# Retention and two feed-forward layers: another load order, other group sizes, and products of zeros between the first blocks

## The chip, the cores and the metric

The kernel runs on one core of a Trainium2 chip. The metric is the device time of one execution in microseconds (us), from repeated runs; the median of three before the change is 877.78 us. A profile of one further execution gives the rows below.

## The reference

```python
scores = scale * np.matmul(q, k.transpose(0, 1, 3, 2))      # q, k, v: 4 x 8 heads x 576 x 64
Dmat = np.where(rel >= 0, gamma[:, None, None] ** rel[None, :, :], 0.0)
x = np.matmul(scores * Dmat[None], v)                       # retention
x = x.transpose(0, 2, 1, 3).reshape(2304, 512)
h = x @ w_in;  x = (h * sigmoid(h)) @ w_out                 # 512 -> 2048 -> 512
h = x @ w_in2; x = (np.maximum(h, 0) + alpha * np.minimum(h, 0)) @ w_out2
```

Everything is float32, but the four weight matrices come as float64.

## The kernel before, in words

**Retention** goes in 18 blocks of 128 tokens, each in two halves of 64 (`att_step`, line 521). A block is loaded in two transfers of 512 KB (`att_load`): q and k, then k and v by token. They go into a ring of five buffers, two of which lie in the buffer `sums` and three in `pack`. `att_prep` scales q and v by powers of gamma, on POOL or VectorE. `att_half` multiplies k with q into the PSUM pair `sc`, and k with v into the running state `total`, in products of 64 x 64 that use a quarter of the array each; the state is copied out after each half (`att<-total`). `att_mask` multiplies `sc` with a mask on VectorE (`att<-sc`, once for each block). `att_out` multiplies states with q and masked scores with v into `xo`; a copy makes the rounded half `xhi` of it and a subtraction the rest, `xlo`.

**The layers** work on products of a rounded high part and a rest: three matmuls for one exact product. A weight tile (512 KB of float64) is loaded into one of two `raw` buffers by `weight` (line 383), and split there by two ScalarE conversions (`top`, `low`), five VectorE instructions, a ScalarE cast and a POOL product (`low<-low,top`). The 2048 hidden features are 16 tiles, taken in groups (`SIZES`, line 31). For each group and each of five token tiles (256, then 512 four times) there are h units (`h_unit`: 12 matmuls into one of three `bank` buffers, then sigmoid or relu, and the split of the result) and, in the first layer, four y units (`y_unit`: three matmuls for each tile of the group, added into `sums` by VectorE from the second group on; in the layer's last group a rounded part and a rest of the sum are made too). The second layer has `out_unit` in place of y.

**The order** of instructions is not that of the code. `Program` records all operations, and `order` lists them with estimated costs: the operation of an engine that is ready and has to be done first (`late`) goes first; TensorE's work is in two queues, retention and layers, whose units stay whole. The result is a fixed order for each engine, and an engine stands still while its next instruction waits. `first` (line 651) puts the blocks between the units of the first group: 6 blocks ahead of the first h unit, the others spread over the rest. The order is issued in two parts, cut at `close_att`; the weights of the first group and of two tiles of the second one belong to the first part.

`gate` (line 374) copies one column of `src` into a buffer about to be loaded, so that the load waits until `src` is there. It holds back blocks 1 to 4 and the first two weights. Before the first block TensorE multiplies zeros (`WARM`, line 33).

Of the kernel before, what the change touches and what calls it, by code (L numbers as in the profile page):

```python
# [18 lines left out]
P = 128  # L19
# [8 lines left out]
NCH = S // C  # L28


SIZES = [[1, 3, 4, 4, 4], [4, 4, 4, 4]]
GROUPS = [(i, range(sum(sizes[:n]), sum(sizes[:n + 1]))) for i, sizes in enumerate(SIZES) for n in range(len(sizes))]
WARM = 12
LEAD = 4
TILES = [256, 512, 512, 512, 512]
RAWS = 2
# [19 lines left out]
class Program:  # L56
# [19 lines left out]
    def __init__(self, nc):  # L76
        self.nc = nc
        for name in self.ENGINES:
            setattr(self, name, self.Engine(self, name))
        self.ops, self.first = [], 0  # L80
        self.writer, self.readers, self.banks = {}, {}, {}
        self.end = {}
        self.free = dict.fromkeys(self.LATENCY, 700.0)
        self.dma, self.was, self.started = 0.0, None, []
        self.queue, self.units, self.joined = "layers", 0, False

    def unit(self, queue, joined=False):

# [19 lines left out]
    def cost(self, engine, out, reads):  # L108
        n = int(np.prod([c for _, c in out.ap[1:]]))
        psum = any(r.space == bass.MemoryType.PSUM for r in reads)  # L110
        if engine == "PE":
            return (n + 32) / 2.4 if reads[0].dtype == F32R else 29 if n == C else 3.4 * n
        if engine == "ACT":
            return (160 if psum else 200) + 0.84 * n + 50 * any(r.dtype != F32 for r in reads)
        if engine == "DVE":
            return 140 + (0.56 if len(reads) < 2 and not psum else 1.075) * n
        if engine == "POOL":
            return 100 + 2.1 * n
        return 450

    def record(self, name, method, args, kwargs, others=()):
        engine = self.ENGINES[name]
        aps = {k: a for k, a in [*enumerate(args), *kwargs.items()] if isinstance(a, bass.AP)}
        key = "out" if "out" in aps else 0
        out = aps.pop(key)
        reads = list(aps.values())
        on_chip = lambda a: type(a.tensor).__name__ == "Tile"
        deps = set()
        i = len(self.ops)
        psum = {}  # L130
        for ap, writes in [(r, False) for r in reads] + [(out, True)]:
            if not on_chip(ap):
                continue
            if ap.space == bass.MemoryType.PSUM:

                for g in self.grains(ap):
                    psum[g] = True
                continue
            for g in self.grains(ap):
                if g in self.writer:  # L140
                    deps.add(self.writer[g])
                if writes:
                    deps.update(self.readers.pop(g, ()))
                    self.writer[g] = i
                else:
                    self.readers.setdefault(g, []).append(i)
        for g in psum:
            runs = self.banks.setdefault(g, [])
            if not runs or runs[-1][0] != engine:
                runs.append((engine, []))  # L150
            if len(runs) > 1:
                deps.update(runs[-2][1])
            runs[-1][1].append(i)
            del runs[:-2]
        deps.discard(i)
        moved = int(np.prod([c for _, c in out.ap])) * np.dtype(mybir.dt.np(out.dtype)).itemsize if engine == "SP" else 0
        shared = engine == "DVE" and all(r.space != bass.MemoryType.PSUM for r in reads)
        self.ops.append((engine, name, method, args, kwargs, deps, self.cost(engine, out, reads), moved,
                         shared, (self.queue, self.units, self.joined),
                         [(self.ENGINES[a], a, b, self.cost(self.ENGINES[a], out, reads)) for a, b in others]))  # L160

    def order(self):

# [7 lines left out]
                at += ops[i][6]  # L171
        for i in reversed(new):
            if ops[i][0] != "PE":
                late[i] = min(late[i], at)
            for d in ops[i][5]:
                if d >= self.first and ops[d][0] != "PE":
                    lag = self.LATENCY[ops[d][0]] if ops[d][0] != ops[i][0] else 0
                    late[d] = min(late[d], late[i] - ops[d][6] - lag)
# [101 lines left out]
def retention_ffn_kernel(ctx: ExitStack, tc: tile.TileContext, qkv, w1, w2, alpha, small, out):  # L280
# [89 lines left out]
    def psum():  # L370

        return rings["bank"].next()

    def gate(dst, src):

        nc.vector.tensor_copy(dst[:, 0:1], src[:, 0:1])


    w_hi, w_lo = {}, {}

    def weight(layer, kind, f):
        if (layer, kind, f) in w_hi:
            return
        raw, top, low, a, hi, lo = (rings[k].next() for k in ("raw", "top", "low", "a", f"w{kind}", f"w{kind}"))
        if len(w_hi) < RAWS:
            gate(raw.bitcast(F32), fac[:, 0])
        nc.sync.dma_start(out=raw, in_=(w1, w2)[layer][kind, f])
        words = raw.bitcast(I32).rearrange("p (n two) -> p n two", two=2)  # L390
        lower, upper = words[:, :, 0], words[:, :, 1]
        nc.scalar.activation(top, upper.bitcast(F32), AF.Copy, scale=2.0 ** -112)
        nc.scalar.activation(low, lower.bitcast(U32), AF.Copy, scale=2.0 ** -52)
        nc.vector.tensor_scalar(out=a, in0=top.bitcast(I32), scalar1=3, scalar2=None, op0=ALU.logical_shift_left)
        nc.vector.scalar_tensor_tensor(out=a, in0=top.bitcast(I32), scalar=-2 ** 31, in1=a, op0=ALU.bitwise_and,
                                       op1=ALU.bitwise_or)
        nc.vector.tensor_scalar(out=top.bitcast(I32), in0=a, scalar1=-2 ** 23, scalar2=None, op0=ALU.bitwise_and)
        nc.scalar.copy(hi, f32(a))
        nc.gpsimd.tensor_tensor(out=low, in0=low, in1=top, op=ALU.mult)
        nc.vector.tensor_tensor(out=f32(a), in0=f32(a), in1=f32(hi), op=ALU.subtract)  # L400
        nc.vector.tensor_tensor(out=lo, in0=f32(a), in1=low, op=ALU.add)
        w_hi[layer, kind, f], w_lo[layer, kind, f] = hi, lo

# [15 lines left out]
        return pack(n)[:, i].rearrange("p (c t) -> p c t", c=NPAIR)  # L421

    def att_load(n):
        if 1 <= n < PACKS:
            for i in (0, 2):
                gate(pack(n)[:, i], fac[:, 0] if n == 1 else pack(n - 2)[:, i + 1])
        nc.sync.dma_start(out=pack(n)[:, 0:2], in_=qkv[n, :, 0:2])
# [93 lines left out]
    def att_step(n):  # L521
# [3 lines left out]
        if m < NBLK:  # L525
            att_load(m)
            att_prep(m)
            att_half(m, 0)
        next(out)
        if m < NBLK:  # L530
            att_half(m, 1)
            att_mask(m)
        for _ in out:
            pass
# [106 lines left out]
            else:  # L641
                e()


    zero = rings["act"].tiles[0]
    nc.gpsimd.memset(zero, 0.0)
    nc.unit("retention")
    for _ in range(WARM):
        nc.tensor.matmul(total[:, 0:P], zero[:, 0:P], zero[:, P:2 * P], start=True, stop=True, skip_group_check=True)
    att_step(-1)  # L650
    first = [(s, u) for s in range(len(TILES)) for u in hs[s] + ys[s]]
    at = 0
# [80 lines left out]
```

## Time and profile before

| | us |
|---|---|
| three timed runs | 876.64, 877.78, 880.19 |
| the profiled execution | 879.05 |
| its span, first to last instruction | 877.2 |
| TensorE busy (PE) | 850.3 (97%) |
| VectorE busy (DVE) | 549.0 (63%) |
| ScalarE busy (ACT) | 380.5 (43%) |
| GpSimd busy (POOL) | 136.5 (16%) |

PE's busy time is taken from records that overlap, so busy is not the same as at its peak. The profile also names, for each 40th of the span, the clock that TensorE was granted: the lower level is half of the upper one. The rows that matter are in the section after the next.

### The profile page before, as it was taken

How to read it: one execution, taken by the hardware profiler on the slowest of the kernel's cores; microseconds unless marked ns; L12 is line 12 of the kernel's file. 1: busy time of each engine (PE TensorE's matmuls, PEld its weight loads, DVE VectorE, ACT ScalarE, POOL GpSimd, SP SyncE). 2: the span in 40 equal slices, each digit the busy share in tenths (PEclk: the TensorE clock that was granted, in tenths of full speed). 3: DMA queues.
4: the chain of work that ended last, by engine and by line, in shares of the span. 5: the costliest groups of instructions: out<-in, count | busy, mean ns of one | idle time of the engine just before them, and what ended most of it. 6: DMA issues, size and time to landing. Idle time of an engine off the chain costs nothing.

```text
span 877.2 us, 14384 instructions
## 1 busy us (share of the span) xinstructions
PE 850.3 (97%) x5956; PEld 715.2 (82%) x5956; DVE 549.0 (63%) x863; ACT 380.5 (43%) x711; POOL 136.5 (16%) x101
## 2 busy tenths in 40 slices
PE   6788999999999999999999999999999999999998
PEld 6666788888888888888888888888888888888887
DVE  4786499783369633995569832984369733954342
ACT  3354474352235422553346644763345533533340
POOL 3575022120003200220002200220002200200000
PEclk6799999999999999999999999999999999999999
DMA  8876032220012100320012100220012100101102
GB/s 310 298 262 206 2 121 73 67 78 1 0 49 96 49 1 0 97 97 1 1 48 97 49 1 1 97 96 1 1 49 97 48 1 1 49 1 48 49 25 96
DMA packets 17490, 58.30 MB, mean 66 GB/s; under 512 B 2064, under 2 KB 2448, under 8 KB 17424
## 3 DMA queue, kind: packets, MB, share of 16 engines
q1 hardware_dynamic: 17424, 57.38, 19.1%
q8 instruction: 46, 0.75, 0.4%
q14 instruction: 20, 0.16, 0.1%
HBM read 52.66 MB, written 4.72 MB: 65 GB/s over the span
## 4 chain that ended last, share of the span: by engine, by line
PE 91%; DVE 4%; issue 2%; DMA 1%; POOL 0%; ACT 0%; SPq 0%; POOLq 0%; DVEq 0%; ACTq 0%
PE bank L276 86%; DVE a L276 2%; PE xo L276 2%; PE sc L276 1%; PE total L276 1%; DMA sums<-in_qkv 1%; DVE act L276 1%; DMA pack<-in_qkv 1%; DVE att L276 0%; DVE xlo L276 0%; DVE top L276 0%; DVE gb L276 0%; POOL pack L276 0%; DVE w L276 0%; DVE g L276 0%
## 5 line engine op out<-in xcount | busy, mean ns | idle before, releaser
L276 PE MATMUL bank<-xhi,w 128*128 128x512 f32 (+1 forms) x880 | 252.0, 371 | 0.7 <-DVE w L276 0.7
L276 POOL TENSOR_TENSOR low<-low,top 128x512 f32<-128x512 f32 x64 | 95.7, 1501 | 600.9 <-DVE top L276 590.7
L276 PEld LDWEIGHTS bank<-xhi,w 128*128 128x128 f32 x880 | 160.7, 190 | 29.0 <-DVE w L276 1.0
L276 PE MATMUL bank<-xlo,w 128*128 128x512 f32 (+1 forms) x440 | 162.9, 370 | 0.0
L276 DVE TENSOR_TENSOR sums<-bank,sums 128x512 f32<-128x512 f32 (+1 forms) x135 | 88.1, 652 | 99.1 <-PE bank L276 98.5
L276 ACT ACTIVATE act<-bank 128x512 f32<-128x512 f32 (+1 forms) x160 | 88.3, 552 | 109.5 <-PE bank L276 105.4
L276 PE MATMUL bank<-xhi,w0b 128*128 128x512 f32 (+1 forms) x400 | 113.2, 368 | 0.0
L276 DVE SCALAR_TENSOR_TENSOR act<-down,nalpha_sb,act 128x512 f32<-128x512 f32 (+1 forms) x80 | 60.2, 753 | 80.0 <-ACT act L276 78.3
L276 PEld LDWEIGHTS bank<-xlo,w 128*128 128x128 f32 x440 | 83.7, 190 | 14.0
L276 ACT ACTIVATE down<-bank 128x512 f32<-128x512 f32 (+1 forms) x80 | 44.3, 554 | 103.7 <-PE bank L276 103.4
L276 PEld LDWEIGHTS bank<-xhi,w0b 128*128 128x128 f32 x400 | 72.6, 188 | 12.6
L276 DVE TENSOR_TENSOR act<-bank,act 128x512 f32<-128x512 f32 (+1 forms) x80 | 50.7, 633 | 50.4 <-ACT act L276 50.3
L276 PE MATMUL bank<-xlo,w0b 128*128 128x512 f32 (+1 forms) x200 | 73.6, 368 | 0.0
L276 DVE TENSOR_TENSOR gb<-act,gb 128x512 fp32r<-128x512 f32 (+1 forms) x79 | 51.9, 659 | 23.4 <-ACT gb L276 23.3
L276 ACT CAST g<-act 128x512 fp32r<-128x512 f32 (+1 forms) x81 | 47.4, 586 | 41.0 <-DVE act L276 41.0
L276 ACT ACTIVATE top<-raw 128x512 f32<-128x512 f32 x64 | 43.3, 676 | 49.7 <-POOL low L276 46.8
L276 PE MATMUL bank<-g,w 128*128 128x512 f32 (+1 forms) x280 | 63.7, 371 | 0.6 <-DVE act L276 0.6
L276 PE MATMUL bank<-gb,w1b 128*128 128x512 f32 (+1 forms) x304 | 62.3, 356 | 0.0
L276 PE MATMUL bank<-w1b,gb 128*128 128x512 f32 (+1 forms) x268 | 62.0, 380 | 0.2 <-DVE gb L276 0.2
L276 ACT CAST gb<-act 128x512 fp32r<-128x512 f32 (+1 forms) x79 | 44.9, 569 | 39.6 <-DVE act L276 39.6
L276 PEld LDWEIGHTS bank<-gb,w1b 128*128 128x128 f32 x304 | 50.7, 189 | 8.2
L276 PEld LDWEIGHTS bank<-w1b,gb 128*128 128x128 f32 x268 | 48.6, 188 | 10.2 <-DVE gb L276 0.6
(74 smaller groups left out, 1189.4 us busy)
## 6 DMA issues: line engine op xcount, KB each, us to landing
raw<-in_w SPq DMA_DIRECT2D x64, 512.0 KB, 3.5
pack<-in_qkv SPq DMA_DIRECT2D x22, 512.0 KB, 5.7
sums<-in_qkv SPq DMA_DIRECT2D x14, 512.0 KB, 5.4
out<-sums SPq DMA_DIRECT2D x17, 256.0 KB, 2.0
out<-sums SPq DMA_DIRECT2D x2, 128.0 KB, 1.7
att<-in_small SPq DMA_DIRECT2D x1, 214.0 KB, 2.6
alpha_sb<-in_alpha SPq DMA_DIRECT2D x1, 8.0 KB, 7.1
```

What stands on the lines that cost most here:

```text
L276: getattr(getattr(self.nc, name), method)(*args, **kwargs)
```

## The change

- **Groups.** The first layer's 16 tiles go in groups of 1, 2, 3, 4, 4 and 2 instead of 1, 3, 4, 4 and 4.
- **Products of zeros.** 36 of 64 columns instead of 12 of 128 ahead of the first block, and four more behind each half of blocks 0 and 1. They read the first `act` buffer and write the third `bank`. The planner counts 110 ns for one.
- **Loads.** The first weight (number 0) is no longer held and gets a due time that puts it first (`DUE`); number 1 is held until block 0's k has landed and is due at 6 us in the planner's time; numbers 2 to 7 are held until `xlo` of blocks 5, 6, 8, 9, 11 and 12 is out (`HOLD`, `LATER`).
- **Gates** are ScalarE copies instead of VectorE copies.

```diff
@@ -28,9 +28,11 @@
 NCH = S // C
 
 
-SIZES = [[1, 3, 4, 4, 4], [4, 4, 4, 4]]
+SIZES = [[1, 2, 3, 4, 4, 2], [4, 4, 4, 4]]
 GROUPS = [(i, range(sum(sizes[:n]), sum(sizes[:n + 1]))) for i, sizes in enumerate(SIZES) for n in range(len(sizes))]
-WARM = 12
+WARM, WARM_BLOCKS = 36, 2
+DUE = {0: -1e5, 1: 6e3}
+LATER = [5, 6, 8, 9, 11, 12]
 LEAD = 4
 TILES = [256, 512, 512, 512, 512]
 RAWS = 2
@@ -83,6 +85,7 @@
         self.free = dict.fromkeys(self.LATENCY, 700.0)
         self.dma, self.was, self.started = 0.0, None, []
         self.queue, self.units, self.joined = "layers", 0, False
+        self.due = float("inf")
 
     def unit(self, queue, joined=False):
 
@@ -109,7 +112,7 @@
         n = int(np.prod([c for _, c in out.ap[1:]]))
         psum = any(r.space == bass.MemoryType.PSUM for r in reads)
         if engine == "PE":
-            return (n + 32) / 2.4 if reads[0].dtype == F32R else 29 if n == C else 3.4 * n
+            return (n + 32) / 2.4 if reads[0].dtype == F32R else 29 if reads[0].ap[0][1] == C else 110
         if engine == "ACT":
             return (160 if psum else 200) + 0.84 * n + 50 * any(r.dtype != F32 for r in reads)
         if engine == "DVE":
@@ -157,7 +160,8 @@
         shared = engine == "DVE" and all(r.space != bass.MemoryType.PSUM for r in reads)
         self.ops.append((engine, name, method, args, kwargs, deps, self.cost(engine, out, reads), moved,
                          shared, (self.queue, self.units, self.joined),
-                         [(self.ENGINES[a], a, b, self.cost(self.ENGINES[a], out, reads)) for a, b in others]))
+                         [(self.ENGINES[a], a, b, self.cost(self.ENGINES[a], out, reads)) for a, b in others],
+                         self.due))
 
     def order(self):
 
@@ -171,7 +175,7 @@
                 at += ops[i][6]
         for i in reversed(new):
             if ops[i][0] != "PE":
-                late[i] = min(late[i], at)
+                late[i] = min(late[i], at, ops[i][11])
             for d in ops[i][5]:
                 if d >= self.first and ops[d][0] != "PE":
                     lag = self.LATENCY[ops[d][0]] if ops[d][0] != ops[i][0] else 0
@@ -371,12 +375,27 @@
 
         return rings["bank"].next()
 
+
+    zero = rings["act"].tiles[0][:, 0:P + C]
+
+    def warm(n):
+        for _ in range(n):
+            nc.tensor.matmul(rings["bank"].tiles[-1][:, 0:C], zero[:, 0:P], zero[:, P:], start=True, stop=True,
+                             skip_group_check=True)
+
     def gate(dst, src):
 
-        nc.vector.tensor_copy(dst[:, 0:1], src[:, 0:1])
+        nc.scalar.copy(dst[:, 0:1], src[:, 0:1])
 
 
     w_hi, w_lo = {}, {}
+
+    def x_low(b):
+        at, n = next((a, m) for a, m in SPANS if a <= b * P < a + m)
+        return f32(acts(xlo, at, n)[:, 0, b * P - at:])
+
+    HOLD = {1: lambda: pack(0)[:, 1]}
+    HOLD.update({2 + i: lambda b=b: x_low(b) for i, b in enumerate(LATER)})
 
 
 
@@ -384,8 +403,9 @@
         if (layer, kind, f) in w_hi:
             return
         raw, top, low, a, hi, lo = (rings[k].next() for k in ("raw", "top", "low", "a", f"w{kind}", f"w{kind}"))
-        if len(w_hi) < RAWS:
-            gate(raw.bitcast(F32), fac[:, 0])
+        nc.due = DUE.get(len(w_hi), float("inf"))
+        if len(w_hi) in HOLD:
+            gate(raw.bitcast(F32), HOLD[len(w_hi)]())
         nc.sync.dma_start(out=raw, in_=(w1, w2)[layer][kind, f])
         words = raw.bitcast(I32).rearrange("p (n two) -> p n two", two=2)
         lower, upper = words[:, :, 0], words[:, :, 1]
@@ -400,6 +420,7 @@
         nc.vector.tensor_tensor(out=f32(a), in0=f32(a), in1=f32(hi), op=ALU.subtract)
         nc.vector.tensor_tensor(out=lo, in0=f32(a), in1=low, op=ALU.add)
         w_hi[layer, kind, f], w_lo[layer, kind, f] = hi, lo
+        nc.due = float("inf")
 
 
 
@@ -421,7 +442,7 @@
         return pack(n)[:, i].rearrange("p (c t) -> p c t", c=NPAIR)
 
     def att_load(n):
-        if 1 <= n < PACKS:
+        if 0 < n < PACKS:
             for i in (0, 2):
                 gate(pack(n)[:, i], fac[:, 0] if n == 1 else pack(n - 2)[:, i + 1])
         nc.sync.dma_start(out=pack(n)[:, 0:2], in_=qkv[n, :, 0:2])
@@ -526,9 +547,13 @@
             att_load(m)
             att_prep(m)
             att_half(m, 0)
+            if m < WARM_BLOCKS:
+                warm(4)
         next(out)
         if m < NBLK:
             att_half(m, 1)
+            if m < WARM_BLOCKS:
+                warm(4)
             att_mask(m)
         for _ in out:
             pass
@@ -641,12 +666,9 @@
             else:
                 e()
 
-
-    zero = rings["act"].tiles[0]
     nc.gpsimd.memset(zero, 0.0)
     nc.unit("retention")
-    for _ in range(WARM):
-        nc.tensor.matmul(total[:, 0:P], zero[:, 0:P], zero[:, P:2 * P], start=True, stop=True, skip_group_check=True)
+    warm(WARM)
     att_step(-1)
     first = [(s, u) for s in range(len(TILES)) for u in hs[s] + ys[s]]
     at = 0
```

SP's queue of loads, from the start; `raw` is a weight, `pack` and `sums` are blocks (blocks 0, 1, 2, 3, 4 lie in `sums`, `pack_111`, `pack_112`, `sums`, `pack_113`, and the ring begins again). Before:

```order
L276 DMA att<-in_small 128x428
L276 DMA sums<-in_qkv 128x1024 x2
L276 DMA pack_111<-in_qkv 128x1024 x2
L276 DMA raw_69<-in_w 128x512
L276 DMA raw_70<-in_w 128x512
L276 DMA pack_112<-in_qkv 128x1024 x2
L276 DMA sums<-in_qkv 128x1024 x3
L276 DMA raw_69<-in_w 128x512
L276 DMA sums<-in_qkv 128x1024
L276 DMA pack_113<-in_qkv 128x1024
L276 DMA raw_70<-in_w 128x512
L276 DMA pack_113<-in_qkv 128x1024
```

SP's queue at the same place, now:

```order
L280 DMA raw_69<-in_w 128x512
L280 DMA att<-in_small 128x428
L280 DMA sums<-in_qkv 128x1024 x2
L280 DMA pack_111<-in_qkv 128x1024 x2
L280 DMA pack_112<-in_qkv 128x1024 x2
L280 DMA sums<-in_qkv 128x1024 x2
L280 DMA pack_113<-in_qkv 128x1024
L280 DMA sums<-in_qkv 128x1024
L280 DMA pack_113<-in_qkv 128x1024
L280 DMA sums<-in_qkv 128x1024
L280 DMA pack_111<-in_qkv 128x1024 x2
L280 DMA raw_70<-in_w 128x512
```

One weight has moved to the front, and the next one stands behind blocks 0 to 6 instead of behind block 1; four weights stood ahead of the last half of block 4, and one does now.

VectorE's queue from the start to block 0's mask (`att<-sc`); `att<-att` makes a table, `a`, `top` and `w` belong to the splitting of a weight. Before:

```order
L276 TENSOR_TENSOR att<-att 128x4x128
L276 COPY pack_111<-att 128x1 x2
L276 COPY raw_69<-att 128x1
L276 COPY raw_70<-att 128x1
L276 TENSOR_TENSOR sums<-sums,att 128x512
L276 TENSOR_TENSOR att<-att 128x4x128
L276 COPY pack_112<-sums 128x1 x2
L276 TENSOR_TENSOR pack_111<-pack_111,att 128x512
L276 TENSOR_TENSOR att<-att 128x4x128
L276 TENSOR_TENSOR att<-sc,att 128x512
```

VectorE's queue at the same place, now:

```order
L280 TENSOR_TENSOR att<-att 128x4x128
L280 TENSOR_SCALAR a_75<-top_71 128x512
L280 SCALAR_TENSOR_TENSOR a_75<-top_71,a_75 128x512
L280 TENSOR_SCALAR top_71<-a_75 128x512
L280 TENSOR_TENSOR a_75<-a_75,w_0_77 128x512
L280 TENSOR_TENSOR att<-att 128x4x128
L280 TENSOR_TENSOR w_1_78<-a_75,low_73 128x512
L280 TENSOR_TENSOR pack_111<-pack_111,att 128x512
L280 TENSOR_TENSOR att<-sc,att 128x512
```

The gates have left VectorE, block 0's q is scaled on POOL, and the whole splitting of the first weight has moved ahead of block 0's mask; its last addition waits for POOL's product `low_73`.

## Rows read from the trace of the kernel before

**Rows 1.** Windows: stretch, its length, busy us of each engine, PEclk, DMA share, GB/s
```profile
10.00:20.00 10.00, 7.56 (x230) 6.84 (x225) 6.55 (x15) 4.91 (x11) 4.81 (x4) 0.50 0.95 368
20.00:30.00 10.00, 6.74 (x223) 6.15 (x216) 5.98 (x12) 3.43 (x9) 5.18 (x5) 0.67 1.03 392
30.00:40.00 10.00, 8.22 (x225) 7.23 (x220) 7.22 (x10) 4.33 (x11) 8.19 (x6) 0.70 0.69 242
40.00:60.00 20.00, 15.65 (x560) 13.17 (x564) 15.40 (x24) 9.67 (x24) 13.50 (x11) 1.00 0.78 263
...
80.00:100.00 20.00, 15.88 (x507) 12.34 (x500) 7.65 (x12) 7.11 (x18) 1.54 (x2) 0.91 0.21 82
...
113.00:150.00 37.00, 37.00 (x187) 31.54 (x186) 34.75 (x57) 21.65 (x39) 10.05 (x7) 1.00 0.30 100
...
200.00:850.00 650.00, 649.59 (x3047) 544.88 (x3046) 395.88 (x613) 281.85 (x511) 66.11 (x44) 1.00 0.12 39
```

**Rows 2.** Timeline of VectorE: start, length, instruction, idle before and its releaser
```profile
12.22 0.69 DVE L276 TENSOR_TENSOR att<-sc,att 128x512 f32<-128x512 f32 x1 [1.01 <-PE total L276]
...
36.41 0.69 DVE L276 TENSOR_TENSOR att<-sc,att 128x512 f32<-128x512 f32 x1 [2.41 <-PE total L276]
...
37.79 0.41 DVE L276 TENSOR_TENSOR act<-bank,act 128x256 f32<-128x256 f32 x1
38.12 0.80 DVE L276 TENSOR_TENSOR w<-a,low 128x512 fp32r<-128x512 f32 x1
39.20 0.69 DVE L276 TENSOR_TENSOR att<-sc,att 128x512 f32<-128x512 f32 x1 [0.28 <-PE total L276]
39.81 0.41 DVE L276 CAST xhi<-xo 128x256 fp32r<-128x256 f32 x1
```

**Rows 3.** Timeline of POOL, the scaling of block 0's v and of block 2
```profile
8.35 1.04 POOL L276 TENSOR_TENSOR sums<-sums,att 128x512 f32<-128x512 f32 x1 [7.09 <-DMA sums<-in_qkv]
...
14.83 2.73 POOL L276 TENSOR_TENSOR pack<-pack,att 128x512 f32<-128x512 f32 x2 [2.72 <-DMA pack<-in_qkv]
```

**Rows 4.** Timeline of TensorE (PE), three gaps ended by "issue"
```profile
25.12 0.21 PE L276 MATMUL total<-sums 64*64 64x64 f32 x1 [2.01 <-issue]
...
47.49 0.21 PE L276 MATMUL total<-pack 64*64 64x64 f32 x1 [1.58 <-issue]
...
85.68 0.21 PE L276 MATMUL total<-sums 64*64 64x64 f32 x1 [2.61 <-issue]
```

**Rows 5.** DMA queues in 83 to 84 us: packets, MB, share
```profile
q8 instruction: 1, 0.02, 5.8%
```

**Rows 6.** The page: instruction queue of the run, and POOL's product in a split
```profile
L276 POOL TENSOR_TENSOR low<-low,top 128x512 f32<-128x512 f32 x64 | 95.7, 1501 | 600.9 <-DVE top L276 590.7
...
q8 instruction: 46, 0.75, 0.4%
```

**Rows 7.** Timeline of TensorE, the products of zeros, first twelve records and last six
```profile
1.31 2.93 PE L276 MATMUL total<-act 128*128 128x128 f32 x12 [1.31 <-POOL act L276]
...
5.31 0.83 PE L276 MATMUL total<-act 128*128 128x128 f32 x6
```

**Rows 8.** Timeline of TensorE, second group's third h unit
```profile
112.67 0.39 PE L276 MATMUL bank<-xhi,w 128*128 128x256 f32 x1 [0.66 <-DVE w L276]
```

**Rows 9.** Groups of VectorE, 118 to 660 us: count, busy us, mean ns, idle before
```profile
L276 DVE TENSOR_TENSOR sums<-bank,sums 128x512 f32<-128x512 f32 x77 | 52.9, 687 | 45.9 <-PE bank L276 45.6
...
L276 DVE SCALAR_TENSOR_TENSOR a<-top,a 128x512 int32<-128x512 int32 x46 | 34.3, 747 | 0.8
...
L276 DVE TENSOR_TENSOR a<-a,w 128x512 f32<-128x512 f32 x26 | 26.9, 1037 | 0.0
...
L276 DVE TENSOR_SCALAR top<-a 128x512 int32<-128x512 int32 x46 | 22.1, 492 | 0.4
L276 DVE TENSOR_SCALAR a<-top 128x512 int32<-128x512 int32 x45 | 20.7, 467 | 0.3
L276 DVE TENSOR_TENSOR w<-a,low 128x512 fp32r<-128x512 f32 x24 | 16.6, 697 | 1.3
```

## The prediction

> **What bounds the kernel now.** I read the table of windows first: from 113 us on TensorE is busy without a break (37.00 of 37 us, later 649.59 of 650), at full clock, so that part is a fixed amount of matmul work [rows 1]. Time can be won only before it, where retention and the first layer's opening group run. There the same table shows another picture: between 10 and 40 us TensorE is busy 6.7 to 8.2 us in ten, and its granted clock is 0.50, 0.67 and 0.70, so it stands at its lower level (1.2 GHz) for all of the first ten and some two thirds of the others, while the DMA engines are 0.95 and 1.03 busy from 10 to 30 us [rows 1].
>
> Next I followed the blocks of retention by VectorE's mask, the instruction `att<-sc` that each block has once. Block 0's starts at 12.22 us, block 4's at 36.41, block 5's at 39.20 [rows 2]: 27 us for five steps, 5.4 us each, while blocks 4 and 5, with their data there, are 2.8 us apart. What the early blocks wait for is seen in POOL's rows: block 0's v is scaled at 8.35 us and block 2's at 14.83, each as soon as a DMA has landed [rows 3]. So the early part is bound by the order in which bytes arrive, with a TensorE at half speed behind that.
>
> The third thing is TensorE's "issue" gaps, in the middle of a run of products and with nothing to wait for: 2.01 us before 25.12, 1.58 before 47.49, 2.61 before 85.68 [rows 4]. A packet of the instruction queue moves in 83 to 84 us, inside the last of them [rows 5], and the run has 46 such packets with 0.75 MB [rows 6], 16 KB each. I read it as TensorE waiting for its own code.
>
> **The change, part by part.**
>
> *Loads.* Before, the queue carries tables, block 0, block 1, two weights, block 2, block 3, then a weight each inside blocks 5 and 4; now one weight stands first and the next comes behind block 6. A weight is 0.52 MB and takes 1.4 us at the 368 to 392 GB/s of 10 to 30 us [rows 1]. Blocks 0 and 1 have one weight more ahead of them: 1.4 us later. Blocks 2 and 3 have one less: 1.4 us earlier. The last half of block 4 had four ahead of it and has one: 4 us earlier.
>
> *Block 0.* Its v lands at 8.35 + 1.4 = 9.75 and is scaled in 1.04 us on POOL [rows 3], by 10.8. POOL's next instruction is the first weight's `low` product, 1.50 us [rows 6], done at 12.3. VectorE's queue has that weight's last addition, which waits for it, and a scaling of block 1 ahead of block 0's mask. VectorE's rows overlap: one of 0.69 us starts at 39.20 and the next at 39.81, one of 0.41 at 37.79 and the next at 38.12 [rows 2], so 0.61 and 0.33 us each in a row. The mask starts at 12.3 + 0.6 + 0.6 = 13.5, against 12.22: 1.3 us late. This is the price of the weight that goes first.
>
> *Blocks 1 to 5.* The first weight is decoded before they start, the second between the masks of blocks 4 and 5, and the others wait for blocks 5, 6, 8 and 9 to be out. So neither the data of blocks 2 to 5 nor decoding should be last any more. A step costs 2.8 us where nothing is missing and 5.4 us on average. I take 3.2, near the first, because the added products should bring the clock up. That is 5 x 3.2 = 16 us, and 0.7 us for six products 256 wide (0.107 us each, half of a full one) of the first h unit, now ahead of block 5, and 1.5 us for one code gap as in rows 4. Block 5's mask is at 13.5 + 16 + 0.7 + 1.5 = 31.7 instead of 39.20: **7.5 us won**. With 2.8 us a step and no code gap it is 11; with 5.4 us a step, in which gaps are contained, it is 41.2, a loss of 2.
>
> *Zero products.* 36 of 64 columns replace 12 of 128 at the start, and 16 more stand behind the halves of blocks 0 and 1. The 12 gave 24 records: the first 12 took 2.93 us, the last 6 took 0.83 [rows 7], so the rate rose within them. A 64-wide record should take half as long, 0.12 us at first and 0.07 at last: 72 records are 8.8 us at the one rate, 5.0 at the other. They start at 1.31 and end between 6.3 and 10.1 us, ahead of block 0's data at 10.8. The 16 are 32 records, 2.2 to 3.9 us of TensorE under the wait for block 0's mask, its state copies and block 1's data; I charge nothing. If that cover is gone they cost these 2.2 to 3.9 us.
>
> *Gates on ScalarE.* The one-column copies that hold loads back move from VectorE to ScalarE. Each waits for a DMA or a scaling, and behind them in ScalarE's queue stand the state copies `att<-total` of blocks 0 and 1, for which TensorE's next half waits. The step of 3.2 us covers some tenths of this; at worst, one landing of 1.4 us in each of these two blocks, it is 2.8 us.
>
> *From block 5 on.* TensorE's queue is nearly the same row by row to the end of the first group, and the decoding of four weights lies in it as before, over blocks 8 to 16 instead of 6 to 13, so partly where VectorE is busy 7.65 of 20 us, from 80 to 100 us [rows 1]. I take 0, with 3 us either way.
>
> *Groups of 1, 2, 3.* The second group no longer needs a third weight tile at its start: the wait of 0.66 us for `w` before 112.67 goes [rows 8]: **0.6 us won**. One group more means 20 more additions into `sums`, 0.69 us each [rows 9]: 13 us of VectorE, beside TensorE's work as long as VectorE has room. The tightest place is the two-tile group at the end of the first layer. By the order, VectorE does from its first h unit to its last 44 instructions of 512 columns (0.61 us) and 12 of 256 (0.33), 31 us, and six decodings of five instructions, 0.467 + 0.747 + 0.492 + 1.037 + 0.697 [rows 9] less 5 x 0.08 of overlap, 3.04 us each: 18 us. TensorE's products there are 120 of its h units, 96 of its own first four tiles' y units and 48 of the group before it: 216 full ones of 649.59 / 3047 = 0.213 us [rows 1] and 48 half-wide ones, 51.2 us. So 49 of 51.2 us, 96%. From 113 to 150 us VectorE was busy 34.75 of 37 us, 94%, and TensorE lost nothing [rows 1]. I charge **1 us**; the lower end is 0, and if the durations did not overlap, both two-tile groups cost up to 13 us (below).
>
> The sum is 7.5 + 0.6 - 1 = 7.1 us. The profiled execution took 879.05 us, its span 877.2; 879.05 - 7.1 = 871.95. The profiled one lies 1.27 us above the median of 877.78, so I expect a median of 871.
>
> *A rule against the rows.* The 40 added matmuls, two products and two weight loads each, put 160 instructions into the stream whose gaps rows 4 show. The Trainium skill (Runtime: NRT & Kernel Launch, Instruction fetch mechanics) says that crossing a 16 KiB block of instructions is mostly hidden. By that rule the 1.5 us for a code gap drop out and the time is 869; the measured gap of 2.61 us with a code packet in it contradicts it, and I keep the 1.5.
>
> **The rivals.**
>
> *Code and clock take the gain back.* Blocks that follow one another faster use up their code faster, and a gap of 2 us can let the clock fall: after the gap of 2.61 us it was 0.91 on average in 80 to 100 us, against 1.00 from 40 to 60 [rows 1, 4]. If each of blocks 1 to 5 pays another 1.2 us for it, the gain at block 5 is 1.5 us and the time 877. For it: the gaps are there already at half clock. Against: after the gap of 1.58 us the clock stayed up.
>
> *VectorE becomes the bound in the two-tile groups: slower.* A y unit there is 6 products, 1.28 us; with three PSUM banks an addition may come 2.6 us late, and three decoding instructions ahead of it are 0.747 + 1.037 + 0.697 = 2.5. It decides once VectorE's load passes TensorE's. With plain durations the last two-tile group has 44 x 0.69 + 12 x 0.41 + 6 x 3.44 = 56 us against 51.2, the other (29 and 8 instructions, seven decodings) 47.4 against 43.6: 8 us; if its queue also stands still behind ScalarE's casts, say 13. With 13 us and the front's gain down to 1.5 the time is 889, with 8 us and the same front 884; I give 885. For it: 96% is close. Against: 94% cost nothing.
>
> *More is won.* With 2.8 us a step, no code gap and the later blocks less crowded on VectorE (3 us), 11 + 3 + 0.6 - 1 gives 13.6 us: 864. Against: rows 4.
>
> **How the numbers follow.** Forecast 0.52 (867 to 875), gain taken back 0.25 (875 to 879), more won 0.15, slower 0.08. Half a per cent, 4.4 us, is about what a measurement here can tell from no change. Below 873.4 lie the third case, four fifths of the first and a remainder of the second: 0.61. Above 882.2 lies the slower case, 0.08; between them 0.31. The range of 862 to 879 leaves out the slower case, the far end of the third and a little of the second, under 0.2.
>
> **What would show it.** Right: block 5's mask at 30 to 33 us and the last block's 6 to 9 us earlier than before; the granted clock at 1.00 from about 16 us on but for single drops after code gaps; in the two-tile groups no more than 1 us of waits of TensorE for `bank`. Wrong: block 0's mask later than 14.5 us, steps of 4 us or more between blocks 1 and 5, a clock at half until 30 us, or waits for `sums` or `act` in the two-tile groups.

## The result, and the profile after

The changed kernel took 886.71 us (median of 4 runs, 886.08 to 887.29) against 877.89 us for the kernel before in the same comparison: ratio 1.0097, 95% interval 1.0075 to 1.0119. It is slower by 8.8 us, where 6.8 us less had been forecast; the time lies above the range of 862 to 879. The profiled execution has a span of 884.9 us.

The windows of the changed kernel come first (columns as in [rows 1]).

```profile
0.00:10.00 10.00, 8.96 (x42) 8.96 (x43) 4.08 (x7) 3.61 (x8) 2.90 (x7) 1.00 0.78 255
10.00:20.00 10.00, 10.00 (x88) 9.65 (x91) 3.12 (x3) 0.66 (x3) 4.17 (x4) 1.00 0.44 157
20.00:30.00 10.00, 10.00 (x174) 9.29 (x170) 3.27 (x5) 1.76 (x7) 1.04 (x1) 1.00 0.59 202
40.00:60.00 20.00, 16.01 (x539) 13.95 (x531) 10.70 (x20) 8.82 (x24) 9.38 (x8) 0.83 0.70 242
113.00:150.00 37.00, 36.60 (x184) 31.01 (x182) 32.80 (x56) 22.21 (x42) 6.21 (x4) 1.00 0.33 114
```

TensorE now has no idle time from 10 to 30 us, yet it runs fewer records there: 88 and 174, where before it ran 230 and 223 [rows 1]. VectorE is down to 3 of 10 us and the DMA engines to 0.44 and 0.59: they wait for TensorE. So the early part has changed its limit, and the engine that is busiest is the one that is late. With what it is busy is seen in the timeline of TensorE, in its rows of the zero products (start, length, instruction, count), the counterpart of [rows 7], with block 0's first product.

```profile
1.04 15.62 PE L280 MATMUL bank<-act 128*128 128x64 f32 x72 [1.04 <-POOL act L280]
16.60 0.37 PE L280 MATMUL sc<-sums 64*64 64x64 f32 x1
17.66 1.97 PE L280 MATMUL bank<-act 128*128 128x64 f32 x8
20.62 1.97 PE L280 MATMUL bank<-act 128*128 128x64 f32 x8
```

The 72 records ahead of block 0 take 15.62 us, 0.217 us each, and end at 16.66 us; the forecast had 5.0 to 8.8 us and an end between 6.3 and 10.1. POOL and VectorE show what stood in the queue behind them. First POOL, the counterpart of [rows 3], then VectorE's masks of blocks 0, 1, 4 and 17, the counterpart of [rows 2].

```profile
7.52 2.72 POOL L280 TENSOR_TENSOR sums<-sums,att 128x512 f32<-128x512 f32 x2 [6.53 <-DMA sums<-in_qkv]
```

```profile
20.74 0.69 DVE L280 TENSOR_TENSOR att<-sc,att 128x512 f32<-128x512 f32 x1 [6.46 <-PE total L280]
27.52 0.69 DVE L280 TENSOR_TENSOR att<-sc,att 128x512 f32<-128x512 f32 x1 [4.76 <-PE total L280]
...
44.57 0.69 DVE L280 TENSOR_TENSOR att<-sc,att 128x512 f32<-128x512 f32 x1 [4.50 <-PE sc L280]
...
103.83 0.69 DVE L280 TENSOR_TENSOR att<-sc,att 128x512 f32<-128x512 f32 x1 [0.48 <-PE sc L280]
```

Block 0's q and v are scaled by 10.24 us; its first product starts at 16.60. Its mask is at 20.74 instead of 12.22, 8.5 us late, and VectorE waited 6.46 us for TensorE. Block 17's mask is 7.5 us late (103.83 against 96.34), and the span ends 7.7 us later (884.9 against 877.2). The groups behind it are nearly as forecast: from 100 us on, TensorE's waits (name of what it waited for, us in all, times, longest) are these.

```profile
PE bank L280 <- DVE act L280: 1.4, 2, 1.0
PE xo L280 <- DVE xlo L280: 1.4, 1, 1.4
PE bank L280 <- DVE gb L280: 0.4, 2, 0.2
```

The wait for `w` [rows 8] is gone.

### The profile page after: what moved, and what is told of

Read it like the earlier page. It is cut to its first block, busy times and chain, and to the rows that moved or that the text cites. A ratio compares the mean times of both kernels' runs of the same rounds, so it can differ in the third digit from the quotient of the medians.

```text
span 884.9 us, 14558 instructions
## 1 busy us (share of the span) xinstructions
PE 866.6 (98%) x6036; PEld 731.4 (83%) x6036; DVE 559.7 (63%) x882; ACT 379.6 (43%) x719; POOL 131.0 (15%) x99
## 4 chain that ended last, share of the span: by engine, by line
PE 94%; DVE 4%; issue 2%; ACT 0%; POOL 0%; DVEq 0%; ACTq 0%; POOLq 0%
PE bank L280 89%; PE xo L280 2%; PE sc L280 2%; DVE a L280 2%; DVE act L280 1%; PE total L280 1%; DVE xlo L280 0%; DVE att L280 0%; DVE gb L280 0%; DVE top L280 0%; DVE w L280 0%; DVE g L280 0%; DVE sums L280 0%; DVE xhi L280 0%; DVE w1b L280 0%
## 5 line engine op out<-in xcount | busy, mean ns | idle before, releaser
L280 POOL TENSOR_TENSOR low<-low,top 128x512 f32<-128x512 f32 x64 | 93.4, 1464 | 594.5 <-DVE top L280 585.5
L280 DVE TENSOR_TENSOR sums<-bank,sums 128x512 f32<-128x512 f32 (+1 forms) x155 | 100.7, 651 | 98.4 <-PE bank L280 96.6
L280 PE MATMUL bank<-gb,w1b 128*128 128x512 f32 (+1 forms) x292 | 67.1, 363 | 1.0 <-DVE act L280 1.0
L280 PEld LDWEIGHTS bank<-w1b,gb 128*128 128x128 f32 x268 | 48.6, 188 | 10.1 <-DVE gb L280 0.6
```

Source lines behind the costliest of these rows:

```text
L280: getattr(getattr(self.nc, name), method)(*args, **kwargs)
```

## Experiments

In the expectations, theory A says that the loss is made by the zero products, which hold TensorE and so delay block 0; the rivals put it into the other parts of the change, the loads and gates or VectorE's load in the two-tile groups. The first four runs compare with a kernel before of 878.84 us, the next four with 877.55, then 878.75 and 877.18. Block times below are those of the mask in VectorE's timeline. The planner's price of a zero product goes with its form in each of these kernels, except in the two of the third experiment, which keep the change's 110 ns.

### The change with the zero products of before

```diff
-WARM, WARM_BLOCKS = 36, 2
+WARM, WARM_BLOCKS = 12, 0
-  nc.tensor.matmul(rings["bank"].tiles[-1][:, 0:C], zero[:, 0:P], zero[:, P:], ...)
+  nc.tensor.matmul(rings["bank"].tiles[-1][:, 0:P], zero[:, 0:P], zero[:, P:2 * P], ...)
```

> The change without its zero products: 12 of 128 columns ahead of block 0 as before, none behind the blocks' halves; loads, gates and groups as changed. Theory A (the 36 products of 64 columns each cost as much as one of 128, 0.21 us a record, and block 0 stands behind them): block 0's mask falls from 20.7 to about 13.5 us, the mask of block 5 comes at 32 to 35 us, and the median is 870 to 876. Rival B (the order of loads and the gates on ScalarE are what is late, the zero products only fill that wait): block 0's mask stays at 18 us or later and the time at 884 to 887. Rival C (the added group of two tiles costs it): the front is early but the time stays above 882.

Measured: 879.57 us, ratio 1.0004 (0.9987 to 1.0021). The loss is gone, and so it lay in the zero products. But nothing is won either, where 870 to 876 had been expected, with block 5's mask at 32 to 35 us. The masks of blocks 0 and 5:

```profile
14.36 0.68 DVE L280 TENSOR_TENSOR att<-sc,att 128x512 f32<-128x512 f32 x1
...
39.97 0.68 DVE L280 TENSOR_TENSOR att<-sc,att 128x512 f32<-128x512 f32 x1
```

Five steps take 25.6 us, 5.1 us each. That is the second thing to explain.

### The zero products alone

The kernel before, with the change's 36 and 16 zero products and nothing else of it.

> The kernel before with nothing but the changed zero products (36 of 64 columns, four behind each half of blocks 0 and 1) and their cost in the planner. Theory A: block 0 starts at 16.6 us or later as in the change, and the time is 886 to 892, so that all of the loss is in this part. Rival B: block 0's data come at 8.4 us here, so the time stays within 2 us of 878.

Measured: 886.83 us, ratio 1.0089 (1.0060 to 1.0118). Block 0's mask stands in the very place that it has in the changed kernel:

```profile
20.74 0.69 DVE L276 TENSOR_TENSOR att<-sc,att 128x512 f32<-128x512 f32 x1 [11.18 <-PE total L276]
```

This edit alone gives 8.0 us, the whole loss within the noise.

### The same zero products with 128 moving columns, and with 64 weight columns

```diff
-  rings["bank"].tiles[-1][:, 0:C], zero[:, 0:P], zero[:, P:]       # the change: 128 weight, 64 moving columns
+  rings["bank"].tiles[-1][:, 0:P], zero[:, 0:P], zero[:, P:2 * P]  # wide: 128 and 128
+  rings["bank"].tiles[-1][0:C, 0:C], zero[:, 0:C], zero[:, P:]     # small weights: 64 and 64
```

> The change with zero products of 128 columns instead of 64, as many of them and in the same places. [...] Rival D (the time of a record goes with its columns, as the prediction had it): they end at 30 us or later and the time is 895 to 905.

> The change with zero products of 64 weight columns instead of 128 (64 moving columns as changed, same number and places). Theory A: the weight load halves, so a record takes 0.11 us at the lower clock; the 72 end at 8.7 us at the latest, ahead of block 0's data, and the clock may rise within them; block 0's mask at about 13.5, median 870 to 877. Rival D: the columns are the same, so nothing changes: end at 16.6 us, 886.

Measured: 877.80 us (ratio 0.9985, 0.9967 to 1.0004) and 877.16 us (0.9985, 0.9964 to 1.0006). The first 72 records in each, wide and then with small weights:

```profile
1.10 10.36 PE L280 MATMUL bank<-act 128*128 128x128 f32 x72 [1.10 <-POOL act L280]
```

```profile
1.04 6.62 PE L280 MATMUL bank<-act 128*64 128x64 f32 x72 [1.04 <-POOL act L280]
```

The masks of block 0 are at 14.05 and 15.08 us, so both kernels lose the delay; 877.80 us is far from rival D's 895 to 905, and 877.16 us is at the upper edge of theory A's 870 to 877. Twice the moving columns make the series shorter, 10.36 instead of 15.62 us. The windows of the zero products' tile show how (columns as in [rows 1], without POOL); first the run with wide products, then the changed kernel, then the first stretch with small weights.

```profile
0.00:5.80 5.80, 4.70 (x23) 4.70 (x24) 0.00 (x0) 0.00 (x0) 1.00 0.65 196
5.80:12.00 6.20, 5.66 (x51) 5.47 (x49) 0.00 (x0) 0.00 (x0) 1.00 0.91 326
```

```profile
1.00:6.00 5.00, 4.96 (x23) 4.96 (x24) 0.00 (x0) 0.00 (x0) 1.00 0.82 244
6.00:16.60 10.60, 10.60 (x51) 10.48 (x50) 0.00 (x0) 0.00 (x0) 1.00 0.69 252
```

```profile
1.00:6.00 5.00, 4.96 (x47) 4.96 (x48) 0.00 (x0) 0.00 (x0) 1.00 0.68 213
```

At first a record takes 4.70 / 23 = 0.204 us with 128 moving columns and 4.96 / 23 = 0.216 with 64: the moving columns don't set it. With 64 weight columns it is 4.96 / 47 = 0.106 us in the same stretch, half as long, and the weight loads (second pair of columns) are busy all the time in each: the weight load sets the record. Then the wide ones fall to 5.66 / 51 = 0.111 us, about half, which I read as TensorE going from its lower level (1.2 GHz) to the higher one (2.4 GHz), though the clock's column reads 1.00 in both stretches; those of the change stay at 10.60 / 51 = 0.208 to their end. Both halves of the forecast's term fell: neither is a 64-wide record half as long, nor did the rate rise ahead of block 0.

### The groups alone, and the loads and gates alone

```diff
-SIZES = [[1, 3, 4, 4, 4], [4, 4, 4, 4]]          # groups alone: the kernel before with this line changed
+SIZES = [[1, 2, 3, 4, 4, 2], [4, 4, 4, 4]]

+DUE = {0: -1e5, 1: 6e3}                          # loads alone: HOLD, DUE, LATER and the copies on ScalarE
+LATER = [5, 6, 8, 9, 11, 12]
-  nc.vector.tensor_copy(dst[:, 0:1], src[:, 0:1])
+  nc.scalar.copy(dst[:, 0:1], src[:, 0:1])
```

> The kernel before with the groups of 1, 2, 3, 4, 4, 2 tiles alone. The forecast's term: 0.6 us won before 112.67 us, 1 us lost in the two-tile groups, so 876 to 879 us against a kernel before of 877.9, and block 5's mask stays at 39 to 40 us. The trace of the changed kernel has 1.4 us of waits for act and 0.4 us for gb behind 100 us, which agrees. Rival, VectorE as the bound in the two-tile groups: 882 us or more, with waits of TensorE for sums, act or bank of several microseconds there.

> The change's loads, due times and gates on ScalarE, with the 12 zero products and the groups of before. The forecast's front (block 0's mask 1.3 us late, blocks 1 to 5 in steps of 3.2 us) would put block 5's mask at 30 to 33 us and the time at 870 to 872 us. Theory now: the steps are 4 to 6 us, because code gaps of 1.5 to 2.5 us, VectorE's scaling and decoding and a TensorE at its lower level are left when the bytes are there; block 5's mask at 38.5 to 40 us, the last block's within 2 us of before, and 877 to 880 us.

Measured: 879.03 us for the groups (ratio 1.0018, 1.0000 to 1.0037), about the forecast's term and not its rival; 886.66 us for the loads (1.0107, 1.0078 to 1.0136), which no theory had expected. Its front is as forecast by the theory: block 5's mask at 39.26, the last at 96.17 against 96.34. The loss comes at 100 to 150 us (waits of TensorE, then windows):

```profile
PE bank L280 <- ACT w L280: 3.1, 1, 3.1
PE bank L280 <- DVE w L280: 2.2, 1, 2.2
```

```profile
100.00:113.00 13.00, 10.81 (x72) 9.05 (x61) 5.59 (x11) 8.30 (x19) 0.00 (x0) 1.00 0.24 81
113.00:150.00 37.00, 33.87 (x160) 28.92 (x161) 32.44 (x52) 18.30 (x32) 10.36 (x7) 0.91 0.32 101
```

TensorE is idle for 3.1 us from 113 to 150 us, where it lost nothing before [rows 1], and for 2.2 us just ahead: a second group of three tiles wants a weight tile that the later loads bring too late (its two gates run on ScalarE at 107.12 and 107.48 us). The gaps are not all of it. The granted clock reads 0.91 there, against 1.00 before, so behind the gaps TensorE stood at its lower level for a while: 160 records instead of 187 are by estimate 27 x 0.213 = 5.8 us, and only 3.1 of them are idle time. So loads and groups are one edit. Alone they cost 9.1 and 1.5 us; together, in the run with the zero products of before, 0.7 us, which its interval doesn't tell from nothing.

### Short zero products, none behind the halves

Both kernels with 52 products of 64 x 64 columns ahead of block 0, the second with the rest of the change.

```diff
+WARM, WARM_BLOCKS = 52, 0
+  nc.tensor.matmul(rings["bank"].tiles[-1][0:C, 0:C], zero[:, 0:C], zero[:, P:], ...)
```

> The kernel before, with 52 zero products of 64 x 64 columns ahead of block 0 in place of the 12 of 128 x 128, and none behind the halves. 104 records: 0.12 us each at first, 0.067 once the rate has risen, so they end near 9.5 us, before block 0's data. If a TensorE at half speed is what costs in the early blocks, 873 to 876 us: its full level is there from the first product of block 0 on. If the early blocks are bound by bytes, code and VectorE, nothing is won: 877 to 879 us, block 5's mask at 38 to 40 us.

> The whole change, but with 52 zero products of 64 x 64 columns ahead of block 0 and none behind the halves. If the early blocks lose by half speed and by the 16 zero products on their chain (about 1.1 us behind each half in the run with 128 columns), 872 to 876 us, with block 5's mask at 35 to 37 us. If code gaps, decoding and VectorE's order set the steps, 877 to 879 us and block 5's mask at 38 to 40 us, as in the runs with small weights and with the zero products of before.

Measured: 879.67 us (ratio 1.0014, 0.9997 to 1.0030) and 881.75 us (1.0040, 1.0019 to 1.0060). The 104 records end at 8.75 and 9.30 us, ahead of block 0, and the early blocks gain little by it: block 5's mask is at 37.77 and 38.88, 1.4 us earlier than in the kernel before and 1.1 us earlier than in the run with the old zero products. The granted clock from 10 to 20 us is 0.72 and 0.83 here, against 0.50 and 0.51 there, so TensorE's level at the start is not the main thing that holds the early blocks. The second time, 881.75, lies above both of its theories; why it is slower than the other runs with mended zero products stays open. The changed kernel's front then shows where TensorE stands still (timeline of TensorE; idle before and what ended it):

```profile
14.86 0.30 PE L280 MATMUL sc<-pack 64*64 64x64 f32 x2 [2.84 <-issue]
21.98 0.39 PE L280 MATMUL xo<-att,pack 64*64 64x64 f32 x11 [2.14 <-issue]
27.16 0.39 PE L280 MATMUL xo<-att,pack 64*64 64x64 f32 x11 [1.05 <-issue]
32.63 0.28 PE L280 MATMUL xo<-att,sums 64*64 64x64 f32 x2 [1.93 <-issue]
```

"Issue" hides two kinds of gap. Block 0's mask ends at 14.08 + 0.68 = 14.76 in this trace, and the product at 14.86 follows it by 0.10 us: that gap is a wait for the mask. (The expectations below count it among the code gaps; without it 5.1 of the 8.0 us, and 12.0 of the 16.3, are left.) The other three follow a packet of the instruction queue, in windows of 0.2 us that start at 19.6, 24.8 and 30.4 us:

```profile
q8 instruction: 1, 0.02, 28.7%
...
q8 instruction: 1, 0.02, 30.0%
...
q8 instruction: 1, 0.02, 30.0%
```

28.7% of 16 engines for 0.2 us is 0.92 us; 19.6 + 0.92 = 20.5, and TensorE goes on 1.4 us later. I sorted all gaps over 0.3 us that the view puts down to "issue", up to 113 us, in thirteen traces in this way: each either ends 0.1 us after a mask or 1.2 to 1.7 us after the end of a packet, and none is left over. The reverse does not hold: 18 packets of this queue come from 10 to 113 us in the kernel before, and six gaps follow one. The gaps of the second kind are 7.9 us in the kernel before, 7.3 after, 9.6 in the change with the old zero products, 12.0 here.

### Fewer products, and half of the bytes

Three limits could set a step: code, bytes, and VectorE's order. A block has 64 products of two records with a weight load each, 256 instructions, and a packet holds 16 KB: about one packet a block, if a packet holds 256 instructions (the gaps come at that spacing, see the last section). Two cuts, each alone and then both, in the kernel of the last run (the diff leaves out that `total` and the state products are cut in the same way, and the zeros in the half that is not loaded). All these kernels leave out products or data of the retention and stand here for their times alone:

```diff
-  for p in range(NPAIR):                                     # fewer products
+  for p in range(0, NPAIR, 2):
-    quarter(two["sc"][rows(i), j, p * C:(p + 1) * C], k[rows(j), p, rows(i)], q[rows(j), p, rows(i)])
+    quarter(two["sc"][rows(i), j, p * C:(p + 2) * C], k[rows(j), p, rows(i)], q[rows(j), p])

-  nc.sync.dma_start(out=pack(n)[:, 0:2], in_=qkv[n, :, 0:2])                # half of the bytes
+  nc.sync.dma_start(out=pack(n)[:, 0:2, 0:m], in_=qkv[n, :, 0:2, 0:m])      # m = DM // 2, DM for block 0
```

> The whole change with 52 small zero products ahead (as the run with them), and with 24 of a block's 64 retention products left out: sc and total of every second pair, and the state products of one of two halves, are not computed for themselves, their neighbours are 128 columns wide in their place. So a block has the same columns to move but 160 of 256 TensorE instructions (0.63 of a 16 KB code packet). Theory, code sets the steps of the early blocks: the 8.0 us of gaps without a wait between the masks of blocks 0 and 5 fall to 3 to 5, block 5's mask comes at 33 to 36 us instead of 38.9, the gaps up to 113 us fall from 16.3 to 6 to 10, and the time from 881.7 to 871 to 876 us. Rival, bytes and VectorE's order set them: other waits take the place of the gaps, block 5's mask at 37 to 39, 878 to 882 us.

> As the run before it, with 24 products of 8 columns a block added (three ahead of each sc product, into the same place, which is then overwritten), so that a block has 64 products and 256 TensorE instructions again. Theory, code: the gaps come back, 12 to 17 us up to 113 us, block 5's mask at 37 to 39 us, 879 to 884 us. Rival, that the run before it gains by fewer products as work and not as code: the gaps stay at its value and the time rises only by the work of the added products, which is 48 records of at most 0.03 us in a block.

> The whole change with 52 small zero products ahead, all 64 products of a block, but of each block from block 1 on only half of its bytes is loaded (0.5 of 1.05 MB; the other half of the buffers is zeros, set once at the start by VectorE and POOL). Theory, bytes set the early steps: POOL no longer waits for pack (2 to 4 us each in the run with all bytes), block 5's mask at 33 to 36 us instead of 38.9, 874 to 878 us instead of 881.7. Theory, code alone: gaps and masks as before, block 5's mask at 37 to 39 us, 879 to 882 us. Theory, each covers the other: also no gain here.

> Half of the bytes, and also 40 of a block's 64 retention products (160 of 256 TensorE instructions, as the run with fewer products, whose block 5 did not come earlier: 38.86 us, 877.6 us). Theory, code and bytes lie beside each other, so that one has to go with the other: block 5's mask at 30 to 34 us and 868 to 873 us. Rival, a third limit (VectorE's order, POOL's scaling of 1.0 to 1.3 us a quarter, the chain from mask to products) sets the steps: block 5's mask at 36 to 39 us and 875 to 878 us.

| kernel | time, us | block 5's mask | code gaps to 113 us |
|---|---|---|---|
| all products, all bytes | 881.75 | 38.88 | 12.0 |
| fewer products | 877.61 | 38.86 | 2.2 |
| half of the bytes | 874.05 | 38.01 | 3.3 |
| both | 869.03 | 35.38 | 0.0 |

The ratios to before are 0.9975 (0.9955 to 0.9995), 0.9958 (0.9940 to 0.9976) and 0.9913 (0.9881 to 0.9945). Neither cut alone moves block 5 by as much as its theory said, and both together bring it to 35.38 us, between the two bounds named for it (34 and 36), with a time inside the 868 to 873 us of "beside each other". After one cut other waits take the place of the gaps. With fewer products it is block 0's mask that is late (waits of TensorE up to 113 us):

```profile
PE sc L280 <- DVE att L280: 5.0, 1, 5.0
```

With half of the bytes it is VectorE's order, which has the decoding of the second weight ahead of a block's `xlo`. First the wait of TensorE, then VectorE's rows in that stretch:

```profile
PE xo L280 <- DVE xlo L280: 9.9, 4, 4.4
```

```profile
26.52 0.43 DVE L280 TENSOR_SCALAR a<-top 128x512 int32<-128x512 int32 x1 [1.34 <-ACT top L280]
26.98 1.42 DVE L280 SCALAR_TENSOR_TENSOR a<-top,a 128x512 int32<-128x512 int32 x1
28.42 1.37 DVE L280 TENSOR_SCALAR top<-a 128x512 int32<-128x512 int32 x1
29.90 1.34 DVE L280 TENSOR_TENSOR a<-a,w 128x512 f32<-128x512 f32 x1
31.16 0.68 DVE L280 TENSOR_TENSOR xlo<-xo,xhi 128x512 fp32r<-128x512 f32 x1
```

With both cuts VectorE has no room left from 20 to 30 us (window, columns as in [rows 1]):

```profile
20.00:30.00 10.00, 6.62 (x164) 5.37 (x164) 9.88 (x13) 4.47 (x11) 7.57 (x7) 1.00 0.55 174
```

So bytes, code and VectorE lie close beside one another in blocks 1 to 5. The time does fall with each cut, by 4.1, 7.7 and 12.7 us between the medians (5.3, 7.3 and 12.4 with each taken against its own kernel before), most of it behind block 5. Half of the bytes also takes away most code gaps, though all products are there: as I read it, the gaps need full data queues as well as short products.

The filled kernel was to tell code from work, and missed both of its theories. It took 892.96 us (ratio 1.0146, 1.0119 to 1.0173) with block 5's mask at 41.25 us. The code gaps are 2.1 us, where the theory of code had 12 to 17; that speaks against it, but not strongly, because the fillers cost more than the 0.03 us allowed for and so stretch the steps (TensorE's groups from 10 to 100 us):

```profile
L280 PE MATMUL sc<-pack 64*64 64x8 f32 x432 | 26.2, 204 | 4.3 <-issue 3.7 <-DVE att L280 0.6
...
L280 PE MATMUL sc<-sums 64*64 64x8 f32 x330 | 18.9, 199 | 3.0 <-issue 1.3 <-DVE att L280 1.1 <-POOL pack L280 0.6
```

762 records in 45.1 us are 0.059 us each. Whether the 4.1 us of "fewer products" are won by less code or by less work stays open.

## Why the prediction was wrong, by its own steps

**The step that failed: "Zero products. ... A 64-wide record should take half as long, 0.12 at first and 0.07 at last".** It took 0.217 us throughout. I scaled the records of [rows 7] by their moving columns. Both shapes load the same 128 weight columns, and that load sets the record, as the runs with 128 moving and with 64 weight columns show. I also took the rise of the rate within [rows 7] as given; here it did not come before block 0. The cost is 15.62 us instead of at most 8.8, an end at 16.66 instead of 10.1 at the latest, and then TensorE's queue: "ahead of block 0's data" was the cover, and it was gone. The forecast gave no price for that case ahead of block 0, though it gave one for the 16 behind the halves, of which each group of eight took 1.97 us, 7.9 us in all against its 2.2 to 3.9. With this edit alone the kernel takes 886.83 us. No rival had it. That the slower rival's 885 us lies close to the measured time is luck: its mechanism, VectorE as the bound in the two-tile groups, is not in the trace, whose waits from 100 us on are 3.2 us in all.

**Also wrong: "Blocks 1 to 5 ... I take 3.2", 7.5 us won.** The run with the old zero products has the rest of the change and takes 879.57 us. From the mask of block 0 to that of block 5 the forecast counts 16 + 0.7 + 1.5 = 18.2 us, and this run takes 25.6: 7.4 us more. Its code gaps there (timeline of TensorE, the counterpart of [rows 4]) are 2.43 + 1.69 + 0.61 = 4.7 us, 3.2 us over the 1.5 charged.

```profile
22.30 0.21 PE L280 MATMUL sc<-pack 64*64 64x64 f32 x1 [2.43 <-issue]
...
27.76 0.26 PE L280 MATMUL total<-sums 64*64 64x64 f32 x1 [1.69 <-issue]
...
37.27 0.21 PE L280 MATMUL sc<-sums 64*64 64x64 f32 x1 [0.61 <-issue]
```

The other 4.2 us are the steps themselves, 4.2 us each without the gaps instead of 3.35 (the h unit's 0.7 included). The 2.8 us between blocks 4 and 5 in the kernel before [rows 2] were not the price of an early block. They were taken at TensorE's higher level (windows of the kernel before):

```profile
30.00:36.00 6.00, 5.21 (x87) 4.68 (x85) 4.00 (x4) 1.91 (x4) 5.82 (x4) 0.50 0.72 260
36.00:40.00 4.00, 3.01 (x149) 2.55 (x144) 3.22 (x6) 2.42 (x7) 2.37 (x3) 1.00 0.65 215
```

The level is not all of it: in the run with wide products the granted clock is 1.00 and 0.97 from 10 to 30 us, and its masks of blocks 0 and 5 are still 24.7 us apart (14.05 and 38.73). That loads and scaling for block 5 had also been done while block 4 waited is my reading, which no run shows. Nor was it true that "neither the data of blocks 2 to 5 nor decoding should be last any more": the last four runs show bytes, code and VectorE's decoding each behind the other.

**Right, in part: the rival "code and clock take the gain back".** Its time of 877 us is near what is left of the change once the zero products are mended (877.16 to 879.57 us in three runs, 881.75 in the fourth), though of its term for code and clock, 1.5 and five times 1.2 us, the code gaps are 4.7 us, and what the clock costs in it no run prices; the rest of the gain went into the steps. The Trainium skill (Runtime: NRT & Kernel Launch, Instruction fetch mechanics) has the crossing of a 16 KiB block of instructions mostly hidden. The trace of before agrees from 113 us on, where 256 instructions last some 25 us and there is no such gap; up to 113 us it has 7.9 us of gaps behind code packets, and there the measurement decides.

**Nearly right: block 0's price.** "13.5 ... 1.3 us late": with the zero products of before its mask is at 14.36, 2.1 us late. The first weight's last addition stands ahead of it, as forecast, but took 1.74 us there instead of the 0.6 counted.

```profile
12.10 1.74 DVE L280 TENSOR_TENSOR w<-a,low 128x512 fp32r<-128x512 f32 x1 [1.16 <-POOL low L280]
```

**Half right: groups.** The 1 us charged for the two-tile groups about stands: the waits for `act` are 0.4 us at 125.7 us and 1.0 us at 447.6 us, while those for `gb` lie in the second layer and were there before. Alone the groups cost 1.5 us, at the edge of the noise. "0.6 won" missed what the edit is for: without it the later loads cost 9.1 us.

**Wrong as a sign: "the granted clock at 1.00 from about 16 us on".** The column reads 1.00 from 0 to 42 us in the changed kernel, and yet TensorE stood at its lower level until about 35 us: the same 32 records of `xo` take 1.13 us and then 0.72.

```profile
31.21 1.13 PE L280 MATMUL xo<-pack,att 64*64 64x64 f32 x32 [0.36 <-DVE xlo L280]
...
35.37 0.72 PE L280 MATMUL xo<-pack,att 64*64 64x64 f32 x32
```

So three of the four signs named for "wrong" came: block 0's mask later than 14.5 us, 5.7 us a step from block 1 to block 4, and a clock at half until 30 us, which only the lengths of records show. What the low level costs beyond the late start no run tells apart, because the runs with wide products and with small weights mend both.

## What to carry to other kernels

A filler product that is to keep an engine busy has to end before the real work can start, by its price in the trace and not by a scaling of one operand: if the size that shrinks is not the one that sets the duration, nothing shrinks. Two steps that follow each other closely after a long wait, at another clock, don't give the price of a step; divide a stretch in which nothing had been saved up. And before an order of loads is changed to take bytes off the path, cut the bytes in an experiment: with half of them the kernel won some 7 us, while its new order won nothing.

## What the runs showed of the hardware beyond that

- The granted clock's column does not tell the level ahead of the first recorded fall: it reads 1.00 for the wide zero products both when they take 0.204 us and when they take 0.111 us, and in the changed kernel up to 42 us, though equal records there get faster only at about 35 us. The spacing of equal records tells it.
- An "issue" gap of TensorE in a stretch of short products is of two kinds, told apart by what ended just before: 0.1 us behind another engine's instruction it is a wait which the view missed; 1.2 to 1.7 us behind a 16 KB packet of the instruction queue I take it for code. That rests on time and place, not on a run that varies code alone: with matmuls and weight loads counted together, these gaps come near the same place modulo 256, at 1.72, 2.71, 3.71, 5.69, 6.68 and 14.62 times 256 records in the kernel before.
- VectorE's decoding is stretched beside a busy POOL: `top<-a` took 1.37 us where POOL worked for 9.22 of 10 us, 0.49 in [rows 9].
